# Attention with one more pipeline stage: probabilities transposed two steps, values taken three steps behind the scores

## The chip, the cores and the metric

One core of a Trainium2 chip runs the whole program. Its engines work side by side, each through its own list of instructions in order: PE (TensorE, matrix products), DVE (VectorE), ACT (ScalarE), POOL (GpSimd) and SP (SyncE, which here only starts transfers). The metric is the device time of one execution in microseconds (us), lower is better. All times below count from the start of the profiled span.

## The reference, cut to what matters

Three stages follow each other: an attention over 4 batches of 8 heads (576 positions, 64 channels) and two mixture-of-experts layers over the 2304 rows it produces. The change touches the first alone.

```python
q_d = q.reshape(B, H, Sd, 4, D).mean(axis=3)        # and k_d, v_d: four positions pooled to one, Sd = 144
out_d = softmax(scale * q_d @ k_d.T) @ v_d           # dense, 144 x 144
out_up = np.repeat(out_d, 4, axis=2)
mask = np.abs(pos[:, None] - pos[None, :]) < 4       # a band of 7
out_local = softmax(where(mask, scale * q @ k.T, -1e9)) @ v
x = (out_up + out_local)                             # then rows of 512 = 8 heads x 64
x = moe(x, ...)                                      # 8 experts, the best two of each row
return moe2(x, ...)                                  # 8 experts, the best one of each row
```

## The kernel before, in words

**The attention.** The 32 heads are done as 16 pairs (`NP = 4 * B`), pair `i` in step `i` of one loop written out in Python. Four heads, two pairs, form a group `g` that shares loads. Of a pair there are: `transposes(i)` (q and k turned on PE, copied from PSUM by ACT, pooled by DVE), `scores(i)` (band scores and pooled scores on PE, into a PSUM tile `pd`), `softmax1(i)`, `softmax_d1(i)`, `softmax_d2(i)` (maxima and subtraction on DVE, exponentials on ACT), `softmax2(i)` (sums and reciprocals on DVE; the products with the reciprocal on POOL and DVE, written to `Pd[i % 2]` for the band and in place to `ped` for the pooled part), `p_transposes(i)` (the probabilities turned on PE, copied by ACT to `pT` and `pdT`, of which there is one buffer each), `values(i)` (the products with v, in the windows `vw` and the pooled `vd`, into PSUM), `scale_d(i)` and `combine(i)` (ACT and DVE write the sum to `xT`).

**The order.** Within step `i` of the kernel before, PE is given: transposes of pair i+1, values of pair i-2, scores of pair i, probability transposes of pair i-1, and in even steps the small transposes of the next group. A product with the identity and the router's weights (`xback_att(t)`, line 955, 8 matmuls) turns 128 rows of x back for tile t and is put before or behind the scores by the two tables `before` and `behind`; ACT copies the result and writes it to DRAM from its own queue (line 980). Every engine keeps the order in which the program gives it its instructions.

**The loads.** All loads of the attention are issued by SP, in program order: `load_vr(g + 1)` (two transfers of 288 KB, v for pooling) and `load_qk(g + 2)` (ten transfers, q and k) in odd steps, `load_vw(g)` (five transfers, the windows of v, about 600 KB) in even steps. `vw` has two buffers, used by groups in turn; `vr` has three tiles, two of them per group; `vd` has two buffers and is filled on POOL by `pool_v(g, c)`.

**What else SP issues there.** At step 12 a fill of the last 640 rows of `x_rows` with zeros (line 1168); at step 14 `ffn.begin`, which loads the first experts' weights (four transfers of 512 KB, lines 676 and 677), and then a fill of the whole `x2_rows` with zeros (line 1176, 5,934 KB). From step 12 on the first router (`route1`) runs in pieces between the attention's DVE operations; when its weights are ready SP writes them (`wb`, line 1021).

**After the loop.** Tiles 13 to 17 of x are turned back (they need `combine` of pair 15), written, and rows are gathered for the first expert; then the expert layers run on PE to the end.

Of the kernel before, what the change touches and what calls it, by code (L numbers as in the profile page):

```python
# [9 lines left out]
F32 = mybir.dt.float32  # L10
# [15 lines left out]
def dap(t, off, ap):  # L26
    return bass.AP(tensor=t.tensor, offset=t.offset + off, ap=ap)
# [17 lines left out]
class Attention:  # L45
# [89 lines left out]
    def load_vr(self, g):  # L135

        S, D, H, nc = self.S, self.D, self.H, self.nc
        b, hh = divmod(g, 2)
        o = (b * H + 4 * hh) * S * D
        vr = [self.sb.tile([72, 4, 4, D], F32, tag="vr", name="vr", bufs=3) for c in range(2)]  # L140
        for c in range(2):
            nc.sync.dma_start(vr[c].rearrange("p h r d -> p h (r d)"),
                              dap(self.v, o + c * 72 * 4 * D, [[4 * D, 72], [S * D, 4], [1, 4 * D]]))
        self.gt[g].update(vr=vr)

    def load_vw(self, g):

        S, D, H, nc = self.S, self.D, self.H, self.nc
        b, hh = divmod(g, 2)
        o = (b * H + 4 * hh) * S * D  # L150
        vw = self.vw[g % 2]
        for i in range(self.NB):
            s0 = i * self.QB - 3
            p0 = max(0, -s0)
            p1 = min(128, S - s0)
            nc.sync.dma_start(vw[p0:p1, i], dap(self.v, o + (s0 + p0) * D, [[D, p1 - p0], [S * D, 4], [1, D]]))
        self.gt[g].update(vw=vw, vd=self.sb.tile([72, 2, 4, D], F32, tag="vd", name="vd"))

    def group(self, g):

# [212 lines left out]
def finish_now(gen):  # L373

    while True:
        try:
            next(gen)
        except StopIteration as e:
            return e.value
# [155 lines left out]
class Items:  # L535
# [87 lines left out]
    def next(self):  # L623

        nc, w, tag, nt = self.nc, self.consts, self.tag, self.nt
        m = w.tile([128, self.most], F32, tag=f"{tag}nm", name="nm")
        j = w.tile([128, self.most], F32, tag=f"{tag}nj", name="nj")
        r = w.tile([128, 1 + nt], F32, tag=f"{tag}nr", name="nr")
        ei = w.tile([128, 1], I32, tag=f"{tag}nei", name="nei")
        nc.vector.tensor_scalar(m, self.ij, self.count, None, op0=ALU.is_equal)  # L630
        for a, src in enumerate([self.ei] + [self.col[:, a] for a in range(nt)]):
            nc.vector.tensor_tensor(j, m, src, op=ALU.mult)
            nc.vector.tensor_reduce(r[:, a:a + 1], j, axis=AX.X, op=ALU.add)
        nc.vector.tensor_copy(ei, r[:, 0:1])
        nc.vector.tensor_scalar(self.count, self.count, 1.0, None, op0=ALU.add)
        return dict(e=ei[0:1], e128=r[:, 0:1], col=[r[:, 1 + a:2 + a] for a in range(nt)])
# [219 lines left out]
def core(ctx, tc, q, k, v, moe_w_gate, moe_w_noise, moe_noise, moe_w1, moe_w2,  # L856
         moe2_modality_id, moe2_w_gate, moe2_modality_bias, moe2_w1, moe2_w2, out):
    nc = tc.nc
    B, H, S, D = q.shape
# [39 lines left out]
    with ExitStack() as actx:  # L899
        att = Attention(actx, tc, q, k, v, identF, xpool)  # L900
# [10 lines left out]
        def load_small():  # L911

            nc.sync.dma_start(gw[:, :, 128:128 + E], dap(moe_w_gate, 0, [[E, 128], [128 * E, 4], [1, E]]))
            nc.sync.dma_start(gw[:, :, 128 + E:], dap(moe_w_noise, 0, [[E, 128], [128 * E, 4], [1, E]]))
            yield
            nc.sync.dma_start(nz, moe_noise.rearrange("(t p) e -> p t e", p=128))
            yield
            nc.sync.dma_start(mid, moe2_modality_id.bitcast(I32).rearrange("(t p w) -> p t w", p=128, w=2))
            yield
            nc.sync.dma_start(g2[:, :, :E], dap(moe2_w_gate, 0, [[E, 128], [128 * E, 4], [1, E]]))  # L920
            nc.sync.dma_start(mb, dap(moe2_modality_bias, 0, [[0, 128], [E, 2], [1, E]]))
# [44 lines left out]
        def flush():  # L966
            while after:
                after.pop(0)()
# [76 lines left out]
        def tick(n=1, pe=False):  # L1045

            if pe:
                wait[0] = False
            while n and back and not wait[0]:
                n -= 1  # L1050
                try:
                    what = next(back[0])
                    wait[0] = what in ("PE", "PE soon") and not pe
                    age[0] = 2 if what == "PE soon" else 0
                except StopIteration:
                    back.pop(0)

        def unblock(lag=0):

            if wait[0]:  # L1060
                if age[0] < lag:
                    age[0] += 1
                else:
                    wait[0] = False
                    tick(1)
# [20 lines left out]
        def places_early():  # L1086

            v, f = (t.rearrange("p (e t) -> p e t", e=E)[:, :NX, :NE0] for t in (tab, fs))
            yield from rt.decode(f, v, rt.padh.rearrange("p (e t) -> p e t", e=E)[:, :NX, :NE0])
            nc.vector.tensor_copy(idx0[:, 0], f)  # L1090

            d = route.tile([128, NX, NE0], F32, tag="hold2", name="hold2")
            nc.vector.tensor_scalar(d, f, float(N), -float(N), op0=ALU.is_ge, op1=ALU.mult)
            yield
            nc.vector.tensor_tensor(idx0[:, 1], d, f, op=ALU.add)
            yield

        att.tick = tick
        NP = 4 * B

        before = {6: 0, 7: 2, 10: 5, 11: 7, 14: 10, 15: 12}
        behind = {6: 1, 7: 3, 9: 4, 10: 6, 11: 8, 13: 9, 14: 11}
        small = load_small()
        finish_now(att.transposes(0))
        att.group(0)
        for i in range(NP + 2):
            g, ph = divmod(i, 2)
            if ph == 1:
                if g + 1 < 2 * B:
                    att.load_vr(g + 1)  # L1110
                if g + 2 < 2 * B:
                    att.load_qk(g + 2)
            if ph == 0 and i and g < 2 * B:
                att.load_vw(g)
            if 3 <= i <= 7:
                next(small, None)
            if i == NP - 1:
                att.pool_v(g, 1)
            if i + 1 < NP:
                if i == 0:  # L1120
                    att.scores(i)
                    att.softmax1(i)
                tr = att.transposes(i + 1)
                next(tr)
            if 1 <= i <= NP:
                att.softmax2(i - 1)
            if i + 1 < NP:
                finish_now(tr)
            if i >= 2:
                att.values(i - 2)  # L1130
                att.scale_d(i - 2)
            flush()
            if i == 12:
                back.append(route1(0, HT, att_bank, nc.vector, nc.gpsimd, hold))
                back.append(places_early())
            unblock(1)
            if i in before:
                xback_att(before[i])
            if 0 < i < NP:
                att.scores(i)  # L1140
            if i >= 2:
                att.combine(i - 2)
            flush()
            tick(2)
            if 1 <= i <= NP:
                pt = att.p_transposes(i - 1)
                next(pt)
            if 0 < i < NP:
                att.softmax1(i)
            if 1 <= i <= NP:  # L1150
                finish_now(pt)
            unblock(1)
            if i < NP:
                att.softmax_d1(i)
                if ph == 0 and g + 1 < 2 * B:
                    att.group(g + 1)
                att.softmax_d2(i)
                for c in ((0,), (1,))[ph] if i > 1 else ((), (0, 1))[ph]:
                    if i < NP - 1:
                        att.pool_v(g, c)  # L1160
            tick(2 if i < NP else 30)
            if i == 9:
                second_bias()
            if i in behind:
                xback_att(behind[i])
            if i == 12:

                nc.sync.dma_start(x_rows[N:].rearrange("(a p) c -> p a c", p=128),
                                  zero[:, None, :].to_broadcast([128, 5, XW]))
            if i == 14:  # L1170
                ffn.begin([dict(e=e, ns=n, w1=moe_w1, w2=moe_w2) for e, n in
                           [(e, EARLY) for e in range(NX)] + [(e, 640 - EARLY) for e in range(NX)]
                           + [(e, 640) for e in range(NX, E)]]
                          + [dict(ns=n, w1=moe2_w1, w2=moe2_w2) for n in [512, 256, 256, 384] + [256] * (STATIC - 1)])

                nc.sync.dma_start(x2_rows.rearrange("(a p) c -> p a c", p=128),
                                  zero[:, None, :YW].to_broadcast([128, NT + 5, YW]))
# [490 lines left out]
```

## Time and profile before

| | |
|---|---|
| time, median of 3 runs | 916.13 us (914.27 to 916.85) |
| profiled execution | 912.5 us, span 910.7 us |
| TensorE clock granted, mean | 0.979 of full |
| busy, share of the span | PE 95%, DVE 60%, ACT 47%, POOL 35% |
| attention | from the start to about 158 us |

A busy share is an average over the whole span; the attention is the first sixth of it and has other limits than the expert layers. Matmuls are pipelined, so a busy PE is not necessarily one at its peak.

### The profile page before, as it was taken

What the parts mean: (1) busy time and instruction counts of PE and PEld (TensorE: products, weight loads), DVE (VectorE), ACT (ScalarE), POOL (GpSimd) and SP (SyncE); (2) the same over time, 40 slices, a digit from 0 to 9 for tenths busy, and PEclk for the clock granted to TensorE, in tenths of its full rate; (3) what the DMA queues carried; (4) which work ended last, traced back from release to release, by engine and by line L of the source; (5) the groups of instructions that cost most, each with busy time, mean ns of one, the idle gap of its engine ahead of it and who ended that gap; (6) DMA issues with size and microseconds to landing.
All of it is one profiled execution on the core that took longest, in us unless ns stands there. A gap on an engine that the chain in (4) does not pass through costs nothing. (4 is left out here: it accounts for less than half of the span.)

```text
span 910.7 us, 18186 instructions
## 1 busy us (share of the span) xinstructions
PE 862.7 (95%) x6775; PEld 758.4 (83%) x6775; DVE 545.7 (60%) x1325; ACT 431.1 (47%) x967; POOL 317.2 (35%) x452
## 2 busy tenths in 40 slices
PE   5998987799999999999999999989989999999995
PEld 4777876798889989999999989978767889999994
DVE  5677798489865544554343443434666877556662
ACT  4576765465554434443342333334324455455552
POOL 7767766255433304224015051050020442222210
PEclk9899998899999999999999999999999999999998
DMA  7968898575776647467137264184424477555650
GB/s 166 182 130 194 198 258 304 179 225 171 249 237 186 152 152 209 118 208 170 65 104 164 83 115 142 47 195 154 151 59 136 142 244 244 186 183 203 221 205 24
DMA packets 158702, 153.83 MB, mean 169 GB/s; under 512 B 74319, under 2 KB 119887, under 8 KB 158608
## 3 DMA queue, kind: packets, MB, share of 16 engines
q1 hardware_dynamic: 142336, 113.33, 40.5%
q0 software_dynamic: 12080, 32.45, 15.4%
q10 hardware_dynamic: 4192, 6.82, 2.1%
q8 instruction: 56, 0.92, 0.4%
q14 instruction: 38, 0.31, 0.1%
HBM read 124.98 MB, written 27.85 MB: 168 GB/s over the span
## 5 line engine op out<-in xcount | busy, mean ns | idle before, releaser
L728 PE MATMUL ph<-xh,whi 128*128 128x256 f32 (+3 forms) x768 | 238.0, 310 | 3.9 <-DVE wlo L689 2.1
L728 PE MATMUL ph<-xl,whi 128*128 128x256 f32 (+3 forms) x768 | 237.1, 309 | 0.5 <-DVE xl L714 0.5
L728 PE MATMUL ph<-xh,wlo 128*128 128x256 f32 (+3 forms) x768 | 237.1, 309 | 0.1
L740 PE MATMUL y<-whi,hh 128*128 128x512 f32 x472 | 191.1, 405 | 0.0
L689 DVE TENSOR_TENSOR wlo<-raw,whi 128x512 fp32r<-128x512 f32 x135 | 93.3, 691 | 158.9 <-ACT whi L688 148.5
L740 PE MATMUL y<-wlo,hh 128*128 128x512 f32 x472 | 187.0, 396 | 0.0
L740 PE MATMUL y<-whi,hl 128*128 128x512 f32 x472 | 186.5, 395 | 0.0
L688 ACT ACTIVATE whi<-raw 128x512 fp32r<-128x512 f32 x160 | 101.0, 631 | 168.0 <-PE y L740 151.7
L728 PEld LDWEIGHTS ph<-xh,whi 128*128 128x128 f32 x768 | 145.6, 190 | 13.4 <-issue 2.5
L728 PEld LDWEIGHTS ph<-xl,whi 128*128 128x128 f32 x768 | 145.6, 190 | 8.4 <-DVE xl L714 1.1
L730 ACT ACTIVATE hh<-ph 128x256 fp32r<-128x256 f32 (+3 forms) x192 | 83.2, 433 | 140.7 <-PE ph L728 130.4
L728 PEld LDWEIGHTS ph<-xh,wlo 128*128 128x128 f32 x768 | 145.9, 190 | 1.9 <-DVE wlo L689 0.4
L731 DVE SCALAR_TENSOR_TENSOR hl<-ph,hh 128x256 fp32r<-128x256 f32 (+3 forms) x192 | 92.3, 481 | 83.8 <-ACT hh L730 81.5
L1210 POOL DMA_INDIRECT x_rows<-y,idx x35 | 58.2, 1662 | 205.5 <-ACT y L1201 105.0
L691 DVE TENSOR_TENSOR wlo<-raw,whi 128x512 fp32r<-128x512 f32 x160 | 119.2, 745 | 12.0 <-ACT whi L690 10.7
L740 PEld LDWEIGHTS y<-whi,hl 128*128 128x128 f32 x472 | 88.8, 188 | 21.2
L740 PEld LDWEIGHTS y<-whi,hh 128*128 128x128 f32 x472 | 89.5, 190 | 13.1 <-DVE y L1203 0.2
L740 PEld LDWEIGHTS y<-wlo,hh 128*128 128x128 f32 x472 | 89.3, 189 | 12.6
L690 ACT ACTIVATE whi<-raw 128x512 fp32r<-128x512 f32 x160 | 98.7, 617 | 0.6 <-DMA raw<-in_moe_w_dram 0.6
L714 DVE TENSOR_TENSOR xl<-pt,xh 128x512 fp32r<-128x512 f32 x59 | 38.6, 687 | 33.0 <-ACT xh L713 32.7
L1210 POOL DMA_INDIRECT out_dram<-y,pi x19 | 20.6, 1084 | 100.6 <-ACT y L1201 44.1
L269 POOL TENSOR_TENSOR Pd<-pe,sm 32x380 f32<-32x380 f32 (+1 forms) x48 | 42.2, 879 | 34.0 <-DVE smd L40 18.3
(304 smaller groups left out, 1072.6 us busy)
## 6 DMA issues: line engine op xcount, KB each, us to landing
raw<-in_moe_w_dram SPq DMA_DIRECT2D x156, 512.0 KB
x_rows<-zero SPq DMA_DIRECT2D x1, 5934.0 KB
vr<-in_v_dram SPq DMA_DIRECT2D x16, 288.0 KB
x2l<-x_rows SPq DMA_DIRECT2D x18, 256.0 KB
qk<-in_q_dram SPq DMA_DIRECT2D x32, 128.0 KB
qk<-in_k_dram SPq DMA_DIRECT2D x32, 128.0 KB
x_rows<-xr ACTq DMA_DIRECT2D x13, 256.0 KB
vw<-in_v_dram SPq DMA_DIRECT2D x24, 128.0 KB
```

What stands on the lines that cost most here:

```text
L269: eng.tensor_tensor(Pd[s, :, W * g:W * g + n], pe[s, :, :n], sm[s, :, None].to_broadcast([W, 2 * NB, n]), op=ALU.mult)
L688: nc.scalar.activation(h1, a, AF.Copy)
L689: eng.tensor_tensor(l1, a, h1.bitcast(F32), op=ALU.subtract)
L690: nc.scalar.activation(hi[:, 1], r2[:, half], AF.Copy)
L691: nc.vector.tensor_tensor(lo[:, 1], r2[:, half], hi[:, 1].bitcast(F32), op=ALU.subtract)
L714: nc.vector.tensor_tensor(xl, p, xh.bitcast(F32), op=ALU.subtract)
L728: nc.tensor.matmul(ps, w[a][:, k], x[b][:, k, s], start=(i == 0), stop=(i == 3 * KD - 1))
L730: nc.scalar.activation(hh[:, s], ps, AF.Relu)
L731: nc.vector.scalar_tensor_tensor(hl[:, s], ps, 0.0, hh[:, s].bitcast(F32), op0=ALU.max, op1=ALU.subtract)
L740: nc.tensor.matmul(p, h[a][:, 128 * j:128 * j + 128], w[b], start=(f == 0 and i == 0), stop=(f == self.FB - 1 and i == 2))
L1210: d = nc.gpsimd.indirect_dma_start(out=dst, out_offset=bass.IndirectOffsetOnAxis(ap=ix, axis=0), in_=y, in_offset=None, **kw)
```

## The change: what it does

The probability transposes move one step later (pair i-2 in step i), and with them values, scaling and combining (pair i-3), so the loop has 19 steps in place of 18. Between `softmax2(i)` and `p_transposes(i)` there now lies a whole step. The tables `before` and `behind` and the start of the router move by one step. `load_vw(g)` moves from step 2g to step 2g+1, behind `load_vr(g + 1)` and `load_qk(g + 2)`; the tile `vd` is therefore taken with `load_vr`. The fills at steps 12 and 14 and `ffn.begin` at step 14 keep their steps. No instruction is added or removed.

```diff
@@ load_vr
-        self.gt[g].update(vr=vr)
+        self.gt[g].update(vr=vr, vd=self.sb.tile([72, 2, 4, D], F32, tag="vd", name="vd"))
@@ load_vw
-        self.gt[g].update(vw=vw, vd=self.sb.tile([72, 2, 4, D], F32, tag="vd", name="vd"))
+        self.gt[g].update(vw=vw)
@@ the loop
-        before = {6: 0, 7: 2, 10: 5, 11: 7, 14: 10, 15: 12}
-        behind = {6: 1, 7: 3, 9: 4, 10: 6, 11: 8, 13: 9, 14: 11}
+        before = {7: 1, 8: 3, 11: 5, 12: 7, 15: 10, 16: 12}
+        behind = {6: 0, 7: 2, 10: 4, 11: 6, 12: 8, 14: 9, 15: 11}
-        for i in range(NP + 2):
+        for i in range(NP + 3):
             g, ph = divmod(i, 2)
-            if ph == 1:
+            if ph == 1 and g < 2 * B:
                 if g + 1 < 2 * B:
                     att.load_vr(g + 1)
                 if g + 2 < 2 * B:
                     att.load_qk(g + 2)
-            if ph == 0 and i and g < 2 * B:
-                att.load_vw(g)
+                if g:
+                    att.load_vw(g)
...
-            if i >= 2:
-                att.values(i - 2)
-                att.scale_d(i - 2)
+            if i >= 3:
+                att.values(i - 3)
+                att.scale_d(i - 3)
             flush()
-            if i == 12:
+            if i == 13:
                 back.append(route1(0, HT, att_bank, nc.vector, nc.gpsimd, hold))
...
-            if i >= 2:
-                att.combine(i - 2)
+            if i >= 3:
+                att.combine(i - 3)
             flush()
             tick(2)
-            if 1 <= i <= NP:
-                pt = att.p_transposes(i - 1)
+            if 2 <= i <= NP + 1:
+                pt = att.p_transposes(i - 2)
                 next(pt)
             if 0 < i < NP:
                 att.softmax1(i)
-            if 1 <= i <= NP:
+            if 2 <= i <= NP + 1:
                 finish_now(pt)
```

## Rows read from the trace of the kernel before

**Rows 1.** The page: engines' busy us, share of the span, instructions.

```profile
PE 862.7 (95%) x6775; PEld 758.4 (83%) x6775; DVE 545.7 (60%) x1325; ACT 431.1 (47%) x967; POOL 317.2 (35%) x452
```

**Rows 2.** Waits of PE, 32 to 142 us (total us, times, longest).

```profile
PE pp L283 <- POOL Pd L269: 8.4, 7, 2.4
```

**Rows 3.** Waits of PE, 142 to 178 us.

```profile
PE pp L283 <- POOL Pd L269: 2.0, 1, 2.0
PE pva L309 <- ACT pdT L294: 1.6, 2, 1.3
PE ppd L292 <- POOL ped L272: 1.1, 1, 1.1
```

**Rows 4.** Windows: length, busy us of PE, PEld, DVE, ACT, POOL; PE clock, DMA share, GB/s.

```profile
100.00:105.00 5.00, 5.00 (x130) 4.47 (x128) 4.29 (x14) 4.18 (x17) 2.46 (x4) 1.00 0.67 163
110.00:115.00 5.00, 4.19 (x125) 3.42 (x122) 4.90 (x14) 2.82 (x10) 4.02 (x5) 1.00 0.61 152
115.00:155.00 40.00, 32.69 (x535) 27.69 (x533) 36.05 (x115) 22.41 (x79) 29.36 (x38) 0.87 0.99 315
120.00:125.00 5.00, 2.58 (x32) 1.79 (x22) 5.00 (x15) 1.07 (x3) 4.41 (x5) 0.99 0.88 253
125.00:130.00 5.00, 5.00 (x41) 4.81 (x42) 4.64 (x15) 3.18 (x14) 1.44 (x2) 0.67 0.88 202
145.00:150.00 5.00, 2.62 (x21) 2.34 (x22) 4.51 (x10) 3.00 (x12) 4.13 (x7) 0.54 1.06 376
155.00:160.00 5.00, 4.86 (x57) 4.38 (x58) 4.83 (x24) 3.30 (x9) 0.00 (x0) 1.00 0.11 18
```

**Rows 5.** Timeline of SP's queue: start us, us, instruction, count.

```profile
101.42 0.84 SPq L142 DMA_DIRECT2D vr<-in_v_dram  x2
...
114.19 2.81 SPq L156 DMA_DIRECT2D vw<-in_v_dram  x5
...
119.06 8.35 SPq L156 DMA_DIRECT2D vw<-in_v_dram  x5
127.47 0.42 SPq L676 DMA_DIRECT2D raw<-in_moe_w_dram  x1
...
129.93 0.85 SPq L1176 DMA_DIRECT2D x_rows<-zero  x1
143.87 3.50 SPq L1021 DMA_DIRECT2D x_rows<-wb  x1
```

**Rows 6.** Transfers in 150 to 154 us: packets by size.

```profile
DMA packets 732, 1.51 MB, mean 378 GB/s; under 512 B 0, under 2 KB 0, under 8 KB 732
```

**Rows 7.** Transfers in 154.5 to 158 us: packets by size.

```profile
DMA packets 982, 0.19 MB, mean 55 GB/s; under 512 B 923, under 2 KB 923, under 8 KB 981
```

**Rows 8.** Waits of SP's queue, 30 to 150 us.

```profile
SPq L129 <- DMA x_rows<-xr: 12.6, 4, 5.8
...
SPq L142 <- POOL vd L181: 1.1, 1, 1.1
```

**Rows 9.** Timeline of PE and DVE: start us, us, instruction, count, idle before.

```profile
139.58 0.33 PE L211 MATMUL pd<-mask,identB 128*128 128x190 bf16 x2
...
148.57 1.28 PE L309 MATMUL pva<-pdT,vd 72*64 72x144 f32 x7 [1.31 <-ACT pdT L294]
...
157.24 0.66 DVE L40 TENSOR_TENSOR xT<-pvm,od 128x488 f32<-128x488 f32 x1
```

**Rows 10.** Groups of PE by line, 85 to 104 us: count, busy us, mean ns.

```profile
L955 PE MATMUL px<-gw,xT 128*128 128x144 f32 (+1 forms) x40 | 5.5, 296 | 0.0
L283 PE MATMUL pp<-gw,Pd 128*128 128x128 f32 x20 | 2.6, 278 | 1.1 <-POOL Pd L269 1.1
L315 PE MATMUL pvm<-pT,vw 128*64 128x122 f32 x36 | 2.4, 267 | 0.0
...
L292 PE MATMUL ppd<-gw,ped 72*72 72x72 f32 x16 | 1.4, 228 | 0.0
```

**Rows 11.** Waits of ACT, 142 to 178 us.

```profile
ACT xh L713 <- DMA x_rows<-xrs: 4.2, 1, 4.2
```

## The prediction, made before the change was run

> **What bounds the kernel now.** I read the page first: PE is busy for 95% of the span [rows 1], so what delays PE anywhere is added to the end almost in full, and the question is what PE waits for in the attention. The list of PE's waits answers that for the stretch in which the change works: up to the last scores PE waits 8.4 us, in seven pieces, for the products `Pd` that POOL writes [rows 2], and in the tail 2.0 us more for `Pd`, 1.1 for `ped` and 1.6 for the copies of the turned probabilities [rows 3]. These are the waits that a whole step between `softmax2` and `p_transposes` can remove. Then the windows, for what else is near its limit: after 120 us DVE is busy 5.00 of 5.00 us, because the first router's operations are mixed in, and PE's clock falls to a mean of 0.67 in 125 to 130, after the stretch in which PE worked only 2.58 of 5 us [rows 4]. Above all, the 16 DMA engines are busy for a share of 0.99 from 115 to 155 us, and from 155 on for 0.11 [rows 4]. So the end of the attention is also the end of a transfer backlog. Last, the timeline of SP's queue: what that backlog is, and in which order it was issued [rows 5].
>
> **Removed waits.** At most the 8.4 us before the last scores, and the slow clock of 125 to 130, 5 x (1 - 0.67) = 1.65 us: 10.0 us. At least the same without the longest wait (2.4 us) and without the clock, if at step 13 DVE, full of router work, is late with the PSUM tiles that the probability transposes need next: 8.4 - 2.4 = 6.0. A second effect: two tiles of x fewer are turned back ahead of the last scores (11 in place of 13, by the two tables), each 8 matmuls; 40 of them take 5.5 us, so 1.1 us a tile [rows 10], 2.2 us. The last scores, at 139.6 now [rows 9], would start at 127 to 131.
>
> **Work added at the end.** Behind the last scores PE used to do two probability transposes and two values; now it does three of each and two more tiles, so what was saved at the front is partly given back. It is the same number of instructions in all.
>
> **What moves and costs nothing.** `ped` and `Pd` are read one step later, `vd` is written by POOL at the end of the step in whose beginning `values` last reads it: in each case the other engine reaches the buffer behind the reader, in program order and by at least a stage, so I put no wait there.
>
> **The moved load.** `load_vw(g)` goes one step back and behind `load_vr(g + 1)` and `load_qk(g + 2)`. In the middle of the attention that shortens its lead: the twelve transfers that now go first took SP from 101.42 to 114.19 [rows 5], 12.8 us, and the use comes one step later, 9.5 us (85 to 104 us holds two steps, 20 transposes of `Pd` at 10 a step [rows 10]): 3.3 us less lead. PE's list has no wait for vw [rows 2], so there was some lead. I take 0, with an upper bound of 3.3 us a group, which the next item would hide.
>
> **The last group is where the order decides.** Before, `load_vw(7)` is issued at step 14 ahead of `ffn.begin` (2 MB of weights) and ahead of the fill of `x2_rows` (5,934 KB); in the timeline vw at 119.06, raw at 127.47, zero at 129.93 [rows 5]. After, it is issued at step 15, behind both. What a transfer behind that fill meets can be read from `wb`: it was issued at 143.87 [rows 5], a small transfer of 64-byte pieces; in 150 to 154 us not one packet under 512 bytes moved, and in 154.5 to 158 there were 923 of them [rows 6, 7]. So it waited over 10 us until the fill had drained. The Trainium skill (DMA: Bandwidth & Descriptors, section Queues, rings and completion order) says that each DMA engine takes the descriptors of one ring in ring order; by that rule the window load cannot pass the fill, and the trace agrees with its 923 packets. The same page (Anatomy of one DMA) gives some 2 us from the last byte to the semaphore, on another path; by it, as an estimate, the result below would be 2 us higher, 922.5; no row here shows it, and the sum is made without it.
>
> When does it land? The bytes up to there are the same in both kernels and only the order differs, so the load that is now last lands when the backlog ends: at 155, less what the engines can catch up. From 100 on they were idle for 5 x 0.33 + 5 x 0.39 + 40 x 0.01 = 4.0 us [rows 4]. So 151 to 155. I take 154, because SP's queue waited for POOL only 1.1 us between 30 and 150 and mostly for landings [rows 8]: it was paced by transfers, which a faster PE does not speed up.
>
> When does PE want it? Probability transposes of a pair take (2.6 + 1.4) / 2 = 2.0 us, values 2.4 / 2 = 1.2 for the windows [rows 10] and some 1.8 with the smaller parts (an estimate), scores about as much as transposes. From the start of the last scores, 127 to 131: scores 2.0, transposes of pair 13 2.0, values of 13 1.8, transposes of 14 2.0, two tiles 2.2, in all 10 us, so `values(14)` at 137 to 141. It waits 13 to 17 us. Behind it on PE stand the probability transposes of pair 15, `values(15)`, the router's matmuls and tiles 13 to 17; DVE stands in `combine(14)`; nothing of the expert layers can start.
>
> **The sum.** Before, from the start of `values(14)` (148.57) to the end of the last `combine` (157.24 + 0.66 = 157.9) passed 9.3 us, at half clock for the most part (0.54) [rows 4, 9]. After the landing the same work remains, less the wait for the last `Pd`, done by then, and `vd`'s part: 1.3 for values, 2.0 transposes, 0.5 for the copy, 2.0 values, 0.8 combine = 6.6 us at full clock, up to 9.3 at half, which an idle PE has brought before. I take 8.3. So 154 + 8.3 = 162.3 in place of 157.9: 4.4 us later. What follows hangs on it one for one: the tiles, their writes, and ACT, which waits 4.2 us for those writes before the first expert's rows can be used [rows 11]. Against the profiled execution 912.5 + 4.4 = 916.9; the median of the runs shown is 3.6 us above that execution, so 916.1 + 4.4 = **920.5 us**. Ends of the unknown parts: landing at 151 and 6.6 us, 157.6, 0.3 earlier than before, 915.8; landing at 155 and 9.3 us, 164.3, 6.4 later, 922.5.
>
> **Rivals.** *The saved waits win (faster).* If the load is not held by the fill, PE sets the end: last scores at 129, then the 18.3 us that passed from them to the last combine, less the waits of the tail (2.0 + 1.1 + 1.6 [rows 3]), plus one more pair's transposes and values and two tiles (2.0 + 1.8 + 2.2): 148.6, 9.3 us earlier, 906.8. For it speaks that all its terms are in the list of waits; against it `wb`. It decides as soon as the load lands before about 147. *No net change.* The backlog also moves forward because PE frees buffers sooner, and the load lands at 149 to 152: within 2.7 us of now, 914 to 919. For it: the idle shares 0.33 and 0.39; against: SP's waits. *ACT is caught as well (slower still).* Four loads of q and k waited 12.6 us for writes of x on ACT's queue that share no data with them [rows 8]: issues are held by landings of earlier transfers. If in turn a write of x on ACT's queue is held until the fill has landed, ACT cannot copy the turned probabilities of pair 14 meanwhile, and their copies, about as long as the transposes that they follow, come on top: 2.0 us, 922.5 for the likeliest landing, 924.5 for the latest. *The change does not remove the waits,* because DVE, at 5.00 of 5.00, takes POOL's place: then PE arrives some us later at the same landing, and the result stays within 1 us of the forecast.
>
> **From the cases to the numbers.** About 0.3% (2.7 us) is what a measurement of this kernel can tell from no change. Forecast 0.55 (920.5, own range 917 to 922.5), ACT caught 0.08, waits not removed 0.05, no net change 0.19, the waits win 0.13. The low end leaves out most of the last case and reaches to the bounds of the even one, the high end adds to the upper bound of 922.5 the 2.0 us of ACT and half of the 3.3 us by which a middle group could come late: 914.5 to 926. Slower 0.55 + 0.08 + 0.03 of the waits not removed = 0.66, same 0.19 + 0.01 = 0.20, faster 0.13 + 0.01 = 0.14.
>
> **What would show it.** In the changed kernel: no or few waits of PE for `Pd`; scores of pair 15 at 127 to 131; SP issuing the last five window loads behind the fill; packets under 512 bytes only from about 150; one wait of PE at line 315 of 10 us or more for vw, with the clock at its lower level behind it; the last combine near 162. I am wrong if that wait is under 7 us, if the scores come no earlier, or if the DMA engines have drained before 148.

## The result and the profile after

The changed kernel took 922.07 us in the median of 9 runs (918.80 to 926.56), the kernel before, beside it, 915.15 (913.50 to 921.67): a ratio of 1.0072, with a 95% interval of 1.0048 to 1.0096. The profiled execution took 920.28 us (span 918.6), against 912.5 (910.7) before: 7.8 us more. The prediction was 920.5 us, in a range of 914.5 to 926.

The page's busy times hardly move [rows 1]; the same work stands elsewhere.

```profile
PE 866.4 (94%) x6775; PEld 760.3 (83%) x6775; DVE 545.4 (59%) x1325; ACT 431.9 (47%) x967; POOL 318.0 (35%) x452
```

Waits of PE from 32 to 142 us (total us, times, longest): `Pd` is gone [rows 2], and a window load and two waits without a releaser ("issue") have come.

```profile
PE pd L217 <- issue: 2.9, 2, 1.9
PE pva L315 <- DMA vw<-in_v_dram: 2.6, 1, 2.6
PE pva L309 <- ACT pdT L294: 2.2, 1, 2.2
PE ppd L292 <- ACT pT L284: 0.2, 1, 0.2
```

PE's timeline of the changed kernel (start us, us, instruction, count, idle before): the front, a middle group, the last two scores with PE's waits around them, the values of pairs 14 and 15, and between these the products for the router's table `tab` (line 532).

```profile
18.64 0.33 PE L211 MATMUL pd<-mask,identB 128*128 128x190 bf16 x2
...
30.49 0.92 PE L166 MATMUL prs<-gw,qk 64*128 64x64 f32 x4 [6.21 <-DMA qk<-in_q_dram]
...
36.33 0.50 PE L211 MATMUL pd<-mask,identB 128*128 128x190 bf16 x2
...
81.77 0.56 PE L315 MATMUL pva<-pT,vw 128*64 128x88 f32 x4 [2.63 <-DMA vw<-in_v_dram]
...
125.59 0.34 PE L211 MATMUL pd<-mask,identB 128*128 128x190 bf16 x2
...
134.10 0.76 PE L309 MATMUL pva<-pdT,vd 72*64 72x144 f32 x6 [2.21 <-ACT pdT L294]
...
137.22 0.33 PE L211 MATMUL pd<-mask,identB 128*128 128x190 bf16 x2
...
147.95 0.85 PE L283 MATMUL pp<-gw,Pd 128*128 128x128 f32 x6 [2.35 <-DVE xT L40]
...
149.81 1.60 PE L309 MATMUL pva<-pdT,vd 72*64 72x144 f32 x8
152.75 0.56 PE L315 MATMUL pva<-pT,vw 128*64 128x88 f32 x4 [1.33 <-DMA vw<-in_v_dram]
...
157.76 0.79 PE L532 MATMUL rbank<-oh,ol 128*128 128x144 f16 x10
...
159.17 1.01 PE L315 MATMUL pvm<-pT,vw 128*64 128x122 f32 x16
```

Step 2 runs ahead (scores at 18.64 us; 28.49 before) and then stands 6.21 us for group 2's queries and keys, so the next scores come at 36.33, where they came at 35.54. The last scores come at 137.22, 2.4 us sooner than before [rows 9], and `values(14)` waits for its windows, but only 1.33 us: PE itself came there at 149.81, later than the 148.57 of before. On the way PE lost most of its lead to DVE: the 2.35 us are for `combine(13)` on DVE, and the copy by ACT for which it waited 2.21 us stood on ACT behind an exponential that had itself waited for DVE:

```profile
133.23 0.52 ACT L233 ACTIVATE pe<-pe 128x380 f32<-128x380 f32 x1 [2.69 <-DVE pe L40]
```

Windows (length; busy us of PE, PEld, DVE, ACT, POOL; PE clock, DMA share, GB/s), to set beside [rows 4], and behind them SP's queue, beside [rows 5]. The last three windows are for later parts of this text.

```profile
115.00:155.00 40.00, 30.75 (x524) 25.82 (x521) 33.10 (x105) 20.10 (x68) 27.68 (x35) 0.89 0.91 287
125.00:130.00 5.00, 3.81 (x114) 2.92 (x111) 5.00 (x15) 2.26 (x7) 4.24 (x5) 1.00 0.92 284
130.00:135.00 5.00, 2.75 (x29) 2.36 (x31) 4.86 (x14) 2.12 (x8) 3.95 (x6) 1.00 1.06 384
145.00:150.00 5.00, 2.43 (x21) 1.74 (x20) 5.00 (x13) 2.67 (x7) 4.79 (x7) 0.98 0.97 308
150.00:155.00 5.00, 3.67 (x29) 2.88 (x29) 1.23 (x7) 0.43 (x2) 2.84 (x5) 0.50 0.39 69
...
160.00:165.00 5.00, 4.09 (x35) 2.97 (x32) 4.83 (x25) 2.51 (x6) 0.30 (x1) 1.00 0.01 3
...
610.00:620.00 10.00, 7.53 (x42) 5.64 (x43) 0.00 (x0) 3.05 (x6) 4.67 (x5) 0.83 0.90 295
670.00:680.00 10.00, 6.21 (x28) 4.91 (x28) 6.36 (x14) 3.57 (x7) 3.12 (x7) 0.83 0.34 100
```

```profile
119.94 1.23 SPq L676 DMA_DIRECT2D raw<-in_moe_w_dram  x1
...
122.83 0.55 SPq L1177 DMA_DIRECT2D x_rows<-zero  x1
126.03 23.74 SPq L156 DMA_DIRECT2D vw<-in_v_dram  x5
149.87 0.37 SPq L1021 DMA_DIRECT2D x_rows<-wb  x1
```

The last window load is issued behind the weights and the fill, over 23.74 us, and the transfers drain nearly 4 us sooner than before (a share of 0.39 in 150 to 155, 1.06 before). DVE has nothing left to spare from 125 to 135 and from 145 to 150 us; PE is busy for about half of 130 to 135 and 145 to 150. Then PE is at the lower of its two clocks (0.50 of full in 150 to 155).

The tail on DVE of the changed kernel (same columns as the timeline):

```profile
148.68 1.36 DVE L527 TENSOR_SCALAR oh<-r_hHI,lchi,r_code 128x144 f16<-128x144 f16 x1
...
158.58 0.30 DVE L1040 TENSOR_TENSOR tab<-tab,rbank 128x144 f32<-128x144 f32 x1 [2.94 <-PE rbank L532]
...
160.41 0.31 DVE L527 TENSOR_SCALAR oh<-r_hHI,lchi,r_code 128x144 f16<-128x144 f16 x1
...
162.20 0.24 DVE L40 TENSOR_TENSOR xT<-pva,od 128x88 f32<-128x88 f32 x1
162.35 0.66 DVE L40 TENSOR_TENSOR xT<-pvm,od 128x488 f32<-128x488 f32 x1
```

`values(15)` is done on PE at 159.17 + 1.01 = 160.18, yet its combine starts at 162.20: on DVE stand ahead of it the router's last eight pairs of one-hots (rows of zeros and ones; 158.81 to 162.2), which came only after the router's `tab`, and for that DVE waited 2.94 us for PE. Before, the same pairs ended as `values(15)` did. The kernel before, on PE:

```profile
149.59 0.35 PE L315 MATMUL pva<-pT,vw 128*64 128x88 f32 x1
...
151.94 0.92 PE L532 MATMUL rbank<-oh,ol 128*128 128x144 f16 x10
```

There the products for `tab` stood ahead of the probability transposes of pair 15; in the changed kernel they stand behind them (157.76). So the window part of `values(14)` starts 3.2 us later than before (149.59, 152.75), and the one-hots add 1.9: the last combine's main part starts 5.1 us later (157.24, 162.35) [rows 9].

### The profile page after: what moved, and what is told of

The parts are those of the page before. It is cut to its first block, busy times and chain, and to the rows that moved or that the text cites. A ratio compares the mean times of both kernels' runs of the same rounds, so it can differ in the third digit from the quotient of the medians.

```text
span 918.6 us, 18181 instructions
## 1 busy us (share of the span) xinstructions
PE 866.4 (94%) x6775; PEld 760.3 (83%) x6775; DVE 545.4 (59%) x1325; ACT 431.9 (47%) x967; POOL 318.0 (35%) x452
## 5 line engine op out<-in xcount | busy, mean ns | idle before, releaser
L688 ACT ACTIVATE whi<-raw 128x512 fp32r<-128x512 f32 x160 | 101.0, 631 | 168.3 <-PE y L740 154.7
L730 ACT ACTIVATE hh<-ph 128x256 fp32r<-128x256 f32 (+3 forms) x192 | 83.3, 434 | 140.7 <-PE ph L728 133.1
```

What stands on the lines that cost most here:

```text
L688: nc.scalar.activation(h1, a, AF.Copy)
L730: nc.scalar.activation(hh[:, s], ps, AF.Relu)
```

## The experiments

The table sets the landmarks of the profiled runs beside the ratios of times to the kernel before (95% interval). "Tiles" is when PE starts tiles 13 to 17, "expert" the first product of the first expert. Each landmark is of one execution, and these lie at different places among their runs: that of e3 was the longest of its twelve (926.53 us, median 922.54), that of e12 the shortest of its twelve (910.88, median 913.63), that of the kernel before (912.5) near its shortest. So a few us between two rows are not a difference of medians.

| run | scores 14, 15 (us) | tiles | expert | ratio |
|---|---|---|---|---|
| before | 131.6, 139.6 | 157.7 | 169.7 | 1 |
| changed | 125.6, 137.2 | 162.5 | 174.7 | 1.0072 |
| e1 fill last | 127.0, 140.7 | 163.7 | 175.4 | 1.0069 [1.0050, 1.0088] |
| e3 before, late load | 133.3, 141.3 | 167.3 | 179.2 | 1.0066 [1.0046, 1.0086] |
| e5 before, late router | 128.7, 141.0 | 157.8, 161.7 | 173.1 | 1.0071 [1.0044, 1.0099] |
| e6 router early | 132.3, 140.2 | 162.1 | 173.5 | 1.0063 [1.0039, 1.0088] |
| e7 both | 134.0, 141.8 | 162.0 | 179.2 | 1.0091 [1.0056, 1.0126] |
| e8 and front | 132.9, 141.4 | 164.0 | 179.4 | 1.0102 [1.0072, 1.0132] |
| e9 even loads | 120.7, 135.2 | 158.1 | 169.8 | 1.0032 [1.0006, 1.0059] |
| e10 and POOL's share | 119.7, 132.9 | 154.7 | 166.3 | 0.9998 [0.9977, 1.0019] |
| e11 before, POOL's share | 138.8, 147.8 | 170.3 | 182.8 | 1.0130 [1.0101, 1.0159] |
| e12 e10 and front | 120.3, 133.2 | 154.5 | 166.2 | 0.9968 [0.9948, 0.9987] |
| e13 no adds | 120.5, 134.5 | 155.3 | 167.2 | 0.9972 [0.9949, 0.9995] |

**One part of the change alone, on the kernel before (e3, e5).**

```diff
 # e3: vd is taken with vr; only group 7's windows move
-            if ph == 0 and i and g < 2 * B:
+            if (ph == 0 and 0 < g < 2 * B - 1) or i == NP - 1:
                 att.load_vw(g)
```

> The kernel before, with one load moved alone: the window values of group 7 asked for at step 15, behind the weights and the fill, instead of at step 14. Load theory: values(14), which begins at 148.6 us there, waits for a landing at 152 to 154 us, and the time is 3 to 6 us above the kernel before (918 to 921). Router theory: the landing is hardly late, VectorE's work is in the same place, and the time stays within 1.5 us of the kernel before.

```diff
-            if i == 12:
+            if i == 13:
                 back.append(route1(0, HT, att_bank, nc.vector, nc.gpsimd, hold))
```

> The kernel before with one number changed: the first router begins at step 13 instead of 12, as in the changed kernel; loads, stages and transposes stay. Router theory: VectorE gets that work 8 us later and is still in it when the last combine comes, so the last tiles come 3 to 6 us later: 918 to 921 us. Load theory: nothing that the last combine waits for is touched before 157 us, and the time stays within 1.5 us of the kernel before.

Both cost what the whole change costs. In e3 the timeline of PE shows the wait that I had forecast:

```profile
150.23 1.52 PE L309 MATMUL pva<-pdT,vd 72*64 72x144 f32 x8 [1.31 <-ACT pdT L294]
158.13 0.56 PE L315 MATMUL pva<-pT,vw 128*64 128x88 f32 x4 [6.38 <-DMA vw<-in_v_dram]
```

The load comes 4 us or more later than I gave it (152 to 154), in the longest execution of the twelve. Packets under 512 bytes, as its own are, number 6 in 148 to 152 us, 1454 in 152 to 156 and 2192 in 156 to 160, the last with those of `wb`, issued at 155.83: it moved once the fill was through. The Trainium skill (DMA: Bandwidth & Descriptors, section Queues, rings and completion order) has descriptors of a ring taken in ring order; the trace agrees. SP was also held while it issued these five loads, from 133.01 to 155.74, and the trace does not tell the one delay from the other. In e5 the last combine stays at 157.12, as before, but the router's second batch of one-hots now comes behind it: PE does tiles 15 to 17 only from 161.71, and the first expert starts 3.4 us later.

```profile
161.71 2.20 PE L955 MATMUL px<-gw,xT 128*128 128x144 f32 x16
```

So either part alone costs that much on the kernel before, the router's not by the last combine, as I had expected, but by the tiles behind it. Neither says yet what the changed kernel loses by which.

**Undoing one part in the changed kernel (e1, e2, e9).**

```diff
 # e1: weights and fill behind step 15
-            if i == 14:
+            if i == 15:
                 ffn.begin([...
```

> The changed kernel with the whole i == 14 block (the first experts' weights and the 5,934 KB fill of x2_rows) put behind step 15, so that the window values of group 7 are asked for ahead of it. If the place of that load behind the fill makes the change slower (my prediction), values(14) finds its data, its wait of 1.3 us and the slow transfers of 146 to 152 us go, and the kernel comes to 914 to 918 us, 4 us or more below the changed one. If the router, begun a step later on a full VectorE, sets the end of the attention, the load was late by no more than it shows (1.3 us) and the time stays within 2 us of the changed kernel, 919 to 922.

The window load goes out ahead of the fill and `values(14)` finds it, but nothing is gained. A middle group now waits 3.7 us in 32 to 142, where it waited 2.6, and PE's two waits for VectorE's work stay as in the changed kernel (2.20 us at 136.05, 2.13 us at 151.41).

```profile
PE pva L315 <- DMA vw<-in_v_dram: 3.7, 1, 3.7
```

e2 moves the window loads back to where they stood before:

```diff
-                if g:
-                    att.load_vw(g)
+            if ph == 0 and i and g < 2 * B:
+                att.load_vw(g)
```

> The changed kernel with the window loads back at the even steps, as before (the tile vd still taken with vr). Load theory: group 7 is asked for ahead of the fill and the middle groups ahead of nothing they were behind before, so both waits on vw (2.6 us at 81.8 and 1.3 us at 152.8) go, and 914 to 917 us follow. Router theory: 919 to 922 us, as the changed kernel, since the steps from 13 on stay bound by VectorE.

This edit put the load ahead of the values that still read the older of the two buffers, so the second pair of each group took its products with a later group's windows, and its 941.67 us (ratio 1.0271) are no time of that order. It shows why the load had to move at all. Put behind those values, it is e9:

```diff
             if i >= 3:
                 att.values(i - 3)
                 att.scale_d(i - 3)
+            if ph == 0 and i and g < 2 * B:
+                att.load_vw(g)
```

> The changed kernel with the window loads asked for in the even steps, behind the values that still read the older buffer: group 7 in step 14, ahead of the fill, the middle groups half a step earlier than behind the queries and keys. Load theory alone: 915 to 918 us. With the router's limit beside it, as the kernel with the fill last showed (no gain): 919 to 923 us, and the waits on vw gone.

Its 919.82 us lie where I put the case of both limits, but the kernel before took 917.59 beside it. By the ratio, 1.0032, about half of the changed kernel's loss is gone; the two intervals just overlap, and the better sign is the trace: the tiles start 4.4 us sooner than there. The waits on vw are gone, those of the middle too. And now the saved waits of the change come to light: PE reaches the scores of step 14 at 120.72, 10.9 us ahead of the kernel before. At step 15 it is 4.4 us ahead, at the tiles 0.4 behind. The windows of e9 say where the lead goes:

```profile
115.00:130.00 15.00, 10.27 (x178) 8.39 (x174) 14.86 (x38) 6.86 (x22) 11.69 (x15) 1.00 0.89 257
130.00:150.00 20.00, 16.68 (x237) 14.75 (x239) 16.72 (x57) 11.89 (x42) 13.61 (x19) 0.86 1.04 372
```

DVE is busy 14.86 of 15 us, PE 10.27; the same two waits of PE are there (2.20 us at 130.80, 1.98 us at 145.96).

**The router back at step 12 (e6, e7, e8).** The first router needs nine tiles turned back, so two of them were put into one step:

```diff
-        before = {7: 1, 8: 3, 11: 5, 12: 7, 15: 10, 16: 12}
-        behind = {6: 0, 7: 2, 10: 4, 11: 6, 12: 8, 14: 9, 15: 11}
+        before = {7: 1, 8: 3, 11: 6, 15: 10, 16: 12}
+        behind = {6: 0, 7: 2, 10: 4, 11: 7, 14: 9, 15: 11}   # and 5 behind 4, 8 behind 7
-            if i == 13:
+            if i == 12:
```

> The changed kernel with the first nine tiles turned back up to one step earlier (4 and 5 behind step 10, 6 in step 11, 7 and 8 behind it) and the first router begun at step 12 again; the loads and the fill stay as in the changed kernel. The runs so far leave two limits side by side: the load behind the fill (alone +0.66%) and the router a step later (alone +0.71%). If both are there, taking the router back only brings PE earlier to the late load: the wait on vw grows from 1.3 to 4 us or more, and the time stays at 918 to 922 us. If the router alone held this kernel, it falls to 913 to 916 us.

> Both remedies together: the tiles and the router a step earlier, and the weights and the fill of x2_rows behind step 15. If the two limits together are the loss, this is the one kernel of the four in which both are gone: the tiles 13 to 17 begin at 154 to 158 us instead of 162.5, and the time is 911 to 916 us, level with the kernel before or up to 4 us below. If the loss has another cause (the steps themselves being longer with three in flight), it stays at 918 us or above.

e7 adds e1's edit, e8 also this one:

```diff
         att.load_vr(0)
-        att.load_vw(0)
...
+                if g == 0:
+                    att.load_qk(2)
                 if g + 1 < 2 * B:
                     att.load_vr(g + 1)
-                if g + 2 < 2 * B:
+                if 0 < g and g + 2 < 2 * B:
                     att.load_qk(g + 2)
-                if g:
-                    att.load_vw(g)
+                att.load_vw(g)
```

> The kernel with both remedies, and at the front the load of group 2's queries and keys put ahead of group 1's vr, with group 0's window values behind them (they are first read at step 3 now). In the changed kernel PE waits 6.2 us for group 2 at 24.3 us and is at half clock to 37.2. If the loads at the front hold the pipeline back, that wait goes and scores(3) comes at 26 to 31 us instead of 36.3; if the gain carries to the last step, the time is 3 to 8 us below the kernel without the front change (905 to 912). If VectorE and the loads of the later steps take it up, the time is that of the kernel without it, within 2 us.

None of the three gained. e7, in which both limits should have been gone, came out at 926.55 us, where its expectation had put another cause, "the steps themselves being longer with three in flight". It does not settle that, because the remedy brought losses of its own. Scores(14) come at 132 to 134 us, 6.7 us or more later than in the changed kernel (in e6 PE waits 2.5 us more for ACT at the tiles of line 955 and 2.4 us for DVE at line 283), and the tiles at 162 and 164: the remedy costs as much as it gives, whether by the two tiles in a step or by the router's work coming among earlier steps was not run apart. So a kernel with the router back at its step and no other loss is missing here. The wait on vw that e6 was to show did not come, since PE was later still. In e7 and e8 the late fill hits what follows; ACT of e7, timeline:

```profile
178.05 0.60 ACT L713 ACTIVATE xh<-pt 128x512 fp32r<-128x512 f32 x1 [8.78 <-DMA x_rows<-xrs]
```

The fill keeps the DMA engines at 1.05 to 175 us, and the last tiles' writes on ACT's queue land behind it: 8.8 us of waiting, where [rows 11] had 4.2. e8 is as slow as e7 within 2 us, its second reading. Its first scores behind the front came sooner (34.3 in place of 35.2), but PE waited 8.7 us in two pieces for windows.

**VectorE's load (e10, e11).** One product per step moves from DVE to POOL:

```diff
-            eng = self.V if g == 0 else nc.gpsimd
-            eng.tensor_tensor(Pd[s, :, W * g:W * g + n], pe[s, :, :n],
+            nc.gpsimd.tensor_tensor(Pd[s, :, W * g:W * g + n], pe[s, :, :n],
```

> The kernel with the window loads in the even steps behind the values, and VectorE's quarter of the division of the local probabilities (the 32x380 product of line 269, 0.76 us on VectorE in each of 16 steps) given to POOL, where the other three quarters take 0.87 us each. If VectorE, full from 115 to 145 us there, holds the last combine back after PE has come 11 us early to scores(14), taking off 0.76 us a step moves the last tiles (158.1 us) forward by 3 to 6 us, as POOL's work has a step to spare now: 912 to 916 us against 919.8. If something else sets that end (the stage's own order, the loads), nothing is gained: 918 to 922.

> The kernel before with the same one edit, the quarter on POOL. There PE waits for POOL's Pd in most steps, with no step to spare: the product that VectorE did beside POOL now stands behind three others on POOL, 0.87 us a step later, in some 12 steps of waiting, and VectorE gains 0.76 us in the steps that it bounds (13 to 16). Stage theory: 4 to 10 us above the kernel before (920 to 926), so that the added stage is what makes the edit possible. Rival: PE's waits on Pd cost nothing at the end, since VectorE sets it, and the edit gains here too: 910 to 914.

On e9 the edit brings the tiles 3.4 us forward and the ratio from 1.0032 to 0.9998 (these intervals overlap too); on the kernel before it costs 1.3%. Its waits of PE in 32 to 142 us, beside [rows 2]:

```profile
PE pp L282 <- POOL Pd L268: 14.7, 11, 3.1
```

So the added stage does what it says: it gives POOL a step to spare, which the kernel before has not. And e10, with three pairs in flight, is level with the kernel before, so a third pair in flight need not cost time.

**The front and a second dose (e12, e13).** e12 is e10 with the lines of e8's edit about `load_qk` alone; e13 adds

```diff
-        self.V.tensor_scalar(sm, sm, 1e-9, None, op0=ALU.add)
...
-        self.V.tensor_scalar(smd, smd, 1e-9, None, op0=ALU.add)
```

> The kernel with even loads and POOL's share, with one more edit at the front: group 2's queries and keys asked for ahead of group 1's vr (whose two issues take 3.1 us of SP's queue), group 0's window values staying where they are. PE waits 5.0 us for group 2 at step 2 there. If what is gained in front carries through steps that PE bounds, scores(3) comes about 3 us sooner than 36.5, the tiles 13 to 17 sooner than 154.7 by 1 to 3 us, and the time is 912 to 915 us, 0 to 0.4% below the kernel before. If VectorE's work from step 13 on sets the end whatever comes before it, the tiles stay at 154 to 155 us and the time level with the kernel before.

> The same, and two small instructions of VectorE taken out of each step: the additions of 1e-9 to the sums sm and smd (0.18 and 0.14 us each, 16 times), so the divisor lacks that constant; the sums hold the exponential of zero, so they are at least 1. The edit would serve the kernel before as well; here it is a second dose for VectorE. If VectorE bounds steps 13 to 16, 0.32 us a step there and the shorter chain in front of POOL bring the tiles 1 to 2 us further forward and the time to 909 to 914 us. If not, within 1 us of the run beside it.

e12 beats both kernels: 913.63 us against 916.18 of the kernel before, run beside it. Scores(3) come at 32.7 us in place of 36.5, but scores(14) at 120.3 (119.7 in e10) and the tiles at 154.5 (154.7): the lead is lost by step 14, as the second reading said, though the median fell by some 0.3%; the two intervals overlap, so that I do not call it the edit's. The second dose for DVE (e13) moves nothing. DVE's tail in e12 shows why less work in the steps no longer helps:

```profile
150.62 0.30 DVE L1039 TENSOR_TENSOR tab<-tab,rbank 128x144 f32<-128x144 f32 x1 [1.92 <-PE rbank L531]
...
154.39 0.65 DVE L40 TENSOR_TENSOR xT<-pvm,od 128x488 f32<-128x488 f32 x1
```

PE had finished `values(15)` at 152.2; the last combine stands behind the one-hots again, and these behind PE's products for `tab`. Putting the combine ahead of them was not tried.

## Why the prediction came out near, point by point

- **The waits for `Pd` go.** Right: none is left in the list of 32 to 142 us.
- **The last scores at 127 to 131.** Wrong: 137.2. The lead of 9.9 us at step 2 was lost to the wait for group 2's load, 6.2 us, with PE at the lower clock after it (0.50 of full in 30 to 35); a middle group cost 2.6 us of waiting; and from the lead of 6.0 us at step 14, 3.6 went in that step, in which DVE was full and PE waited 2.2 us behind it. With the loads mended (e9) the lead at step 14 was 10.9 us, in the order of the 10.0 plus 2.2 that I had; at step 15 it was 4.4.
- **Middle groups: 0, at most 3.3.** The bound was the better figure: 2.63 us for one group, and 4.4 us at the tiles between the changed kernel and e9, for all the window loads together. e1 took away the last group's part alone and gained nothing, though with 3.7 us of waiting in a middle group.
- **Group 7 behind the fill, landing at 151 to 155.** Right in the changed kernel (152.75), and e3 shows the late load alone. Its small packets came sooner than the 150 that I gave (586 of them in 145 to 148). But I argued that SP is paced by transfers: the fill went out at 122.83, 7.1 us earlier than before [rows 5], 5.6 earlier than in e3, and the landing was 5.4 us ahead of e3's. The full list of SP's waits, of which [rows 8] shows two lines, also has some 14 us put down to PE on lines 129 and 156; I passed over them.
- **PE waits 13 to 17 us there.** This is the step that failed; the wait was 1.33 us. By my own test (under 7 us) I was wrong on what holds PE. What held PE in its place was VectorE, with waits of 2.21 and 2.35 us, so that it came to `values(14)` at 149.8. That was my rival "DVE takes POOL's place", with a chance of 0.05 and a price of at most 1 us. The two limits lay 1.3 us apart, and that I had not worked out: the number came near by luck as far as this step goes. e1 shows that removing the last load's place alone leaves the other.
- **8.3 us from the landing to the end of the last combine.** It was 163.0 - 152.75 = 10.3, the difference being the router's one-hots ahead of that combine (2.0 us). The late landing that I took (154) made up for it, two errors against each other: I had 162.3, the trace 163.0.
- **Passed on one for one.** To the first expert, yes: 5.0 us. The profiled execution lost 2.9 us more in the expert layers, which I had not forecast.
- **ACT caught too.** No sign of it: ACT's wait for the tiles' writes was 4.3 us, 4.2 before [rows 11].

The sum was 4.4 us on the attention; it was 4.8 at the tiles and 5.0 at the first expert.

**Open.** What the two waits "issue" (2.9 us) at line 217 are. Why e10, with the first expert 3.4 us sooner, is only level with the kernel before: its profiled expert layers took 745.7 us from the first product to the end, 741.0 in the execution profiled before, and that one, at 912.5, lay near the shortest of its runs. In the changed kernel the last two windows above, 610 to 620 and 670 to 680, show part of it: the granted clock is 0.83 in each, which is at most 10 x 0.17 = 1.7 us of work lost each time; the kernel before lost at most 10 x (0.12 + 0.05) = 1.7 us in all, in 660 to 680 (0.88 and 0.95; 1.00 in 610 to 620). What decides on these stretches in the other runs was not tested.

## What to carry to other kernels

A wait that is removed is worth only what the next limit leaves: here two, a load behind a large fill and a full VectorE, lay so close that taking away the first alone in the changed kernel showed nothing, while each of the two delays alone on the kernel before cost the whole. (The router's delay was not taken away without other losses.) So try suspected costs on the kernel before as well, and look at which engine's list the last instruction of the stage stands in, and behind what. A load that has to be moved for a buffer's sake should go to the first place behind the last reader, not to the next convenient step.

## What the runs showed of the hardware

The same one-hot instruction on DVE of the changed kernel (line 527, in the tail above) takes 0.31 us at 160.41, in a window in which POOL is busy 0.30 of 5 us, and 1.36 us at 148.68, where POOL is busy 4.79 of 5. In e10, where POOL has more to do, ten of them between 80 and 150 us take 791 ns in the mean, in e9 550. So part of what was moved from DVE to POOL came back as longer DVE instructions. The Trainium skill (Trainium Architecture — The Big Picture, section What this means for kernel authors) says that VectorE and GpSimd share a port pair that one of them locks; the times agree, but no run here isolates the port.
